# The hand-over from attention to the experts, written out in one order

## The chip, the cores and the metric

The kernel runs on one core of a Trainium2 chip. TensorE (PE) multiplies matrices into PSUM, VectorE (DVE), ScalarE (ACT) and GpSimd (POOL) do the rest, and SyncE (SP) issues most transfers; POOL issues the indirect ones. Each engine works through its own instructions in program order. The metric is the device time of one execution in microseconds (us), lower is better.

## The reference: windowed attention, then a mixture of experts

```python
scores = scale * np.matmul(q, k.transpose(0, 1, 3, 2))     # q, k, v: 8 x 8 heads x 576 x 64
mask = (rel >= 0) & (rel < 64)                             # each row sees itself and 63 before it
attn = softmax(np.where(mask, scores, -1e9));  x = attn @ v  # -> x: 4608 tokens x 512
logits = (x / |x|) @ (emb / |emb|).T / tau                 # 8 experts
expert_idx = np.argmax(logits, axis=1);  gate_w = softmax(logits)[expert_idx]
for e in range(8):                                         # w1[e]: 512 x 1024, w2[e]: 1024 x 512
    h = np.maximum(x[mask] @ w1[e], 0.0)
    out[mask] = gate_w[mask, None] * (h @ w2[e])
```

All is in 32-bit floats.

## The kernel before

Attention runs over 36 tiles of 128 tokens (`T` = 0 to 35). A tile passes through a row of links, and `stages(s)` writes one link of each of several tiles: `scores(s)`, then `own_scores` (ACT), `all_scores` and `maxima` (DVE), `less_max` (POOL), `exponentials` (ACT) of tile s; `attn_transposes` (PE), `attn_own` and `attn_prev` (DVE) of tile s-1; `values` (PE) and `x_out` (DVE) of tile s-2; `x_transposes` (PE), `xT_evac` and `squares` (ACT) of tile s-3; `logits` (PE) of tile s-4. Per group of two or four tiles there follow `logits_out` and `choose` (DVE), the running count of tokens per expert (POOL), `ranks` (PE) and `ranks_out` (DVE). `place(T)` (POOL) then scatters the tile's 128 rows of x into a table in DRAM, sorted by expert. It reads the row buffer `xbuf[T % 8]`, so the next tile that uses this buffer may write to it only when that scatter has landed; the first such write is `tokens(T)` (POOL) or `x_out(T)`.

The experts work on slots of 128 rows, in 21 fixed steps `g` of two slots each (`F`) or one (`H`). Slots 0 and 1 (step 0) and 2 and 3 (step 1) are known to belong to expert 0 and need only the first 24 and 32 tiles. All later slots depend on the counts of all 36 tiles: `cnt = counts(...)`, then some fifty small DVE operations, `slot_rows`, which give `meta` (the expert of a step) and `where` (the rows of a slot). Only then can SP issue `load1(2)`, the 2 MB of `w1` for step 2, and after it the rows of slots 4 and 5 (`load_x`).

A slot's x is loaded (`xb`), turned by DVE (`xt`, `STREAM_TRANSPOSE` x4), rounded by ACT (`xh`), and POOL takes the rest (`xl = xt - xh`). A weight is split in the same way: ACT makes `w1h` from `w1raw`, and DVE `w1l`. `layer1(g, f)` is a piece of 12 matmuls, 128 x 128 by 128 x 256, for f = 0 to 7; two pieces fill a PSUM bank `ph`, from which ACT makes `hh` and DVE `hl`. `layer2(g)` is 48 matmuls with 512 columns.

In what follows the end of attention is the stretch from the last full stage to the first piece of step 2. Before, stage 35 is the last call of `stages`; then `x_parts(0)` and `x_parts(1)`, the links that were left, pieces of step 0 between some of them, the rest of step 0, all of step 1's first layer, `layer2(0)`, and then `step(1)`, whose first work on PE is `layer1` of step 2.

Of the kernel before, what the change touches and what calls it, by code (L numbers as in the profile page):

```python
# [9 lines left out]
F32 = mybir.dt.float32  # L10
# [11 lines left out]
P = 128  # L22
# [63 lines left out]
def attention_moe(ctx, tc, q, k, v, emb, tau, w1, w2, kc, kt, out):  # L86
# [5 lines left out]
    stage_a, stage_p, stage_q = ExitStack(), ExitStack(), ExitStack()  # L92
    ap = stage_a.enter_context(tc.tile_pool(name="ap", bufs=2, side="right"))
    aq = stage_q.enter_context(tc.tile_pool(name="aq", bufs=2))
    psq = stage_q.enter_context(tc.tile_pool(name="psq", bufs=1, space=PSUM))
    psa = stage_p.enter_context(tc.tile_pool(name="psa", bufs=1, space=PSUM, side="right"))

# [17 lines left out]
    turned, score = (psq.tile([P, 2, 512], F32, name=nm) for nm in ("turned", "score"))  # L115
# [101 lines left out]
    vb = [ap.tile([P, 4, NB, D + 1], F32, name=f"v{i}", bufs=1) for i in range(2)]  # L217
# [147 lines left out]
    def choose(G):  # L365
# [13 lines left out]
        for i in range(n):  # L379
            T = a + i  # L380
            nc.gpsimd.tensor_tensor(out=acc[:, T + 1], in0=acc[:, T], in1=oh[:, i], op=ALU.add)
# [11 lines left out]
    def counts(T, name):  # L393

        pn = cnv
        nc.tensor.matmul(pn, lhsT=ones, rhs=acc[:, T], start=True, stop=True)
        o = const.tile([P, E], F32, name=name)
        nc.vector.tensor_copy(o, pn)
        return o
# [83 lines left out]
    def stages(s):  # L483
# [60 lines left out]
        for G in ending(3):  # L544
            choose(G)
        for n, i in todo[1:]:
            keep_chunk(n, i)
# [151 lines left out]
    def shared_rows():  # L699

        ovv = misc[:, 136:136 + SLOTS]
# [25 lines left out]
    def x_parts(a):  # L727

        b, t = xb.pop(a), take("xt")
        o = t.rearrange("p (c t i) -> p t c i", c=4, i=32)  # L730
        bv = b.rearrange("p (t c j) -> p t c j", t=4, j=32)
        for k in range(4):
            nc.vector.transpose(o[:, k], bv[:, k])  # L733
        g, j = POS[a]
        if j == 0:
            xp[g] = take("xh"), take("xl")
        xh, xl = (x[:, :, j * P:(j + 1) * P] for x in xp[g])
        t = t.rearrange("p (c n) -> p c n", c=4)
        nc.scalar.copy(xh, t)  # L739
        nc.gpsimd.tensor_tensor(out=xl, in0=t, in1=xh.bitcast(F32), op=ALU.subtract)  # L740

# [93 lines left out]

    def hidden(g, part):

        if part == 0:
            hp[g] = take("hh"), take("hl")
        hh, hl = (x[:, part * 512:(part + 1) * 512] for x in hp[g])  # L840
        p = ph.pop((g, part))
        nc.scalar.activation(hh, p, AF.Relu)  # L842
# [293 lines left out]
```

## Time and profile before

| what | us |
|---|---|
| median of 3 runs | 677.48 (676.59 to 681.18) |
| the profiled execution | 673.52 |
| its span, first to last instruction | 671.7 |
| PE busy in the span | 638.5 (95%) |
| DVE busy | 463.2 (69%) |
| ACT busy | 392.1 (58%) |
| POOL busy | 204.1 (30%) |

The page divides the span into slices and engines; the trace behind it lists each instruction with its start and length. A matmul's length is modelled and overlaps the next, so what a row of matmuls costs is read from start to start. The share "PEclk" is the TensorE clock that was granted: 1.00 is 2.4 GHz and 0.50 is 1.2 GHz. Idle time is put down to the instruction that ended it.

### The profile page before, as it was taken

The numbers are of one execution on the slowest core, as the hardware profiler recorded it, in microseconds if no ns is written. First come the engines' busy times: TensorE is split into PE (matmuls) and PEld (weight loads), VectorE is DVE, ScalarE is ACT, GpSimd is POOL, SyncE is SP. The second block draws the span as 40 slices with busy tenths as digits, with TensorE's granted clock in tenths as the row PEclk, the third lists the DMA queues.
The fourth block names the chain that finished last, engine by engine and source line by source line (L and its number), as shares of the span: only waits on it lengthen the run. The fifth ranks groups of instructions, "written<-read, shape, count | busy, mean of one in ns | idle before, by whom it ended". The sixth has DMA issues, their size and how long they took to land.

```text
span 671.7 us, 19526 instructions
## 1 busy us (share of the span) xinstructions
PE 638.5 (95%) x7564; PEld 570.9 (85%) x7564; DVE 463.2 (69%) x978; ACT 392.1 (58%) x591; POOL 204.1 (30%) x243
## 2 busy tenths in 40 slices
PE   8899999999978999999999999999999999999991
PEld 7788888887867979988998899998989998999881
DVE  2688898889887885667656877567665776647630
ACT  4587787777653444465546765546565466546640
POOL 0223555544463422222221332222122322231111
PEclk9999999999988999999999999999999999999996
DMA  8999988988372358884688689784797967767221
GB/s 232 228 249 271 257 236 218 229 230 198 103 239 76 129 138 309 280 274 157 228 267 273 220 262 298 218 292 161 250 309 225 291 235 233 238 220 268 101 71 35
DMA packets 122021, 146.86 MB, mean 219 GB/s; under 512 B 52406, under 2 KB 85046, under 8 KB 121921
## 3 DMA queue, kind: packets, MB, share of 16 engines
q1 hardware_dynamic: 115024, 125.19, 63.2%
q0 software_dynamic: 6000, 19.18, 7.5%
q8 instruction: 61, 1.00, 0.7%
q10 hardware_dynamic: 896, 1.18, 0.6%
q14 instruction: 40, 0.32, 0.1%
HBM read 123.09 MB, written 23.20 MB: 218 GB/s over the span
## 4 chain that ended last, share of the span: by engine, by line
PE 71%; DVE 13%; DMA 6%; issue 4%; SPq 2%; ACT 1%; POOL 0%; ACTq 0%; POOLq 0%; DVEq 0%
PE ph L833 28%; PE po L882 28%; PE pair L297 2%; PE turned L183 2%; PE ph L860 2%; PE back L334 2%; PE score L245 2%; DMA raw<-in_q 2%; DVE xr L317 2%; PE pair L302 2%; DVE aP L286 2%; DVE aO L282 1%; PE misc L351 1%; DMA raw<-in_k 1%; SPq L159 1%
## 5 line engine op out<-in xcount | busy, mean ns | idle before, releaser
L833 PE MATMUL ph<-xh,w1l 128*128 128x256 f32 x576 | 164.2, 285 | 1.7 <-DVE w1l L145 1.5
L833 PE MATMUL ph<-xh,w1h 128*128 128x256 f32 x576 | 164.2, 285 | 0.0
L833 PE MATMUL ph<-xl,w1h 128*128 128x256 f32 x576 | 163.7, 284 | 0.0
L882 PE MATMUL po<-w2h,hl 128*128 128x512 f32 x312 | 121.9, 391 | 0.0
L882 PE MATMUL po<-w2h,hh 128*128 128x512 f32 x312 | 121.9, 391 | 0.0
L882 PE MATMUL po<-w2l,hh 128*128 128x512 f32 x312 | 121.8, 390 | 0.0
L843 DVE SCALAR_TENSOR_TENSOR hl<-ph,hh 128x512 fp32r<-128x512 f32 x78 | 53.5, 689 | 98.8 <-ACT hh L842 98.8
L892 POOL DMA_INDIRECT out<-o,rest x39 | 49.8, 1277 | 218.7 <-ACT o L891 205.4
L833 PEld LDWEIGHTS ph<-xh,w1l 128*128 128x128 f32 x576 | 111.3, 193 | 2.5 <-DVE w1l L145 2.5
L145 DVE TENSOR_TENSOR w2l<-w2raw,w2h 128x1024 fp32r<-128x1024 f32 x80 | 94.7, 1220 | 26.7 <-ACT w2h L142 25.1
L833 PEld LDWEIGHTS ph<-xh,w1h 128*128 128x128 f32 x576 | 111.1, 193 | 1.0 <-issue 0.2
L833 PEld LDWEIGHTS ph<-xl,w1h 128*128 128x128 f32 x576 | 111.2, 193 | 0.6
L142 ACT CAST w2h<-w2raw 128x1024 fp32r<-128x1024 f32 x80 | 81.6, 1049 | 47.6 <-PE po L882 35.1
L145 DVE TENSOR_TENSOR w1l<-w1raw,w1h 128x1024 fp32r<-128x1024 f32 x80 | 94.1, 1234 | 10.9 <-ACT w1h L142 10.6
L740 POOL TENSOR_TENSOR xl<-xt,xh 128x512 fp32r<-128x512 f32 x39 | 50.3, 1294 | 111.6 <-ACT xh L739 111.6
L842 ACT ACTIVATE hh<-ph 128x512 fp32r<-128x512 f32 x78 | 45.8, 594 | 58.5 <-PE ph L833 51.0
L142 ACT CAST w1h<-w1raw 128x1024 fp32r<-128x1024 f32 x80 | 78.0, 1048 | 0.0
L882 PEld LDWEIGHTS po<-w2h,hl 128*128 128x128 f32 x312 | 58.6, 188 | 12.3
L882 PEld LDWEIGHTS po<-w2l,hh 128*128 128x128 f32 x312 | 58.6, 188 | 11.8
L882 PEld LDWEIGHTS po<-w2h,hh 128*128 128x128 f32 x312 | 58.7, 188 | 11.7
L265 POOL TENSOR_TENSOR sm<-sm,st 128x512 f32<-128x512 f32 x36 | 37.4, 1040 | 68.4 <-DVE sums L314 22.9
L739 ACT CAST xh<-xt 128x512 fp32r<-128x512 f32 x39 | 24.2, 620 | 56.7 <-DVE xt L733 55.8
(175 smaller groups left out, 1007.8 us busy)
## 6 DMA issues: line engine op xcount, KB each, us to landing
w1raw<-in_moe_w SPq DMA_DIRECT2D x80, 512.0 KB
w2raw<-in_moe_w SPq DMA_DIRECT2D x80, 512.0 KB
xb<-xs SPq DMA_DIRECT2D x156, 64.0 KB
raw<-in_q SPq DMA_DIRECT2D x64, 144.0 KB
v<-in_v SPq DMA_DIRECT2D x64, 144.0 KB
raw<-in_k SPq DMA_DIRECT2D x56, 144.0 KB
xs<-xr SPq DMA_DIRECT2D x12, 264.0 KB
rest<-xs SPq DMA_DIRECT2D x39, 8.0 KB
```

The lines of the kernel that those rows point to most:

```text
L142: nc.scalar.copy(hi[c], raw[c])
L145: eng.tensor_tensor(out=lo[c], in0=raw[c], in1=hi[c].bitcast(F32), op=ALU.subtract)
L183: nc.tensor.transpose(to[:, j // 3, j % 3 * I:(j % 3 + 1) * I], rl[n][:, j, 2 * i:2 * i + 2].rearrange("p h d -> p (h d)"), ident[:I, :I])
L245: nc.tensor.matmul(score[64 * z:64 * z + 64, hp, (u + 1) * P - w:(u + 1) * P], lhsT=qT[b % 2][pr, u, at:at + WIN], rhs=kT[b % 2][pr, u, at ...
L265: nc.gpsimd.tensor_tensor(out=t, in0=t, in1=st.pop(T).unsqueeze(2).to_broadcast([P, 8, WIN]), op=ALU.subtract)
L739: nc.scalar.copy(xh, t)
L740: nc.gpsimd.tensor_tensor(out=xl, in0=t, in1=xh.bitcast(F32), op=ALU.subtract)
L833: nc.tensor.matmul(o, lhsT=ww[c][:, f * P:(f + 1) * P], rhs=xx[:, c, :n], start=(c == 0 and i == 0), stop=(c == 3 and i == 2))
L842: nc.scalar.activation(hh, p, AF.Relu)
L843: nc.vector.scalar_tensor_tensor(out=hl, in0=p, scalar=0.0, in1=hh.bitcast(F32), op0=ALU.max, op1=ALU.subtract)
L882: nc.tensor.matmul(po[a], lhsT=xx[:, f, at], rhs=ww[f // 2][:, f % 2], start=(f == 0 and i == 0), stop=(f == 7 and i == 2))
L892: d = nc.gpsimd.indirect_dma_start(out=out, out_offset=bass.IndirectOffsetOnAxis(ap=tok, axis=0), in_=o, in_offset=None, bounds_check=N - ...
```

## The change

Stage 35 is no longer written by `stages`; the loop ends at stage 34, and all that follows up to `layer2(0)` stands in one order written by hand, in which pieces of `layer1(0)` lie between the links of tiles 33 to 35. Helpers are split so that their parts can be placed alone: `x_parts` into `x_turned`, `x_hi` and `x_lo`, `hidden` into `hidden_hi` and `hidden_lo`, `choose` into `choose` and `count`, `counts` into `sum_counts` and `counts`. The first `xh`, `xl` and the two `xt` have memory from the start, `load_x(0)` and `load_x(1)` are issued one stage earlier, the PSUM banks of `turned` are given up first and those of `score` next, and the memory of V goes to `w2l`. The tile of the shared-rows sum moves to a `ph` bank inside `layer2(0)`.

```diff
-    stage_a, stage_p, stage_q = ExitStack(), ExitStack(), ExitStack()
+    stage_a, stage_v, stage_p, stage_q, stage_s, stage_t = (ExitStack() for _ in range(6))
...
-    for t in range(NT):
+    for name, shape, dtype in (("xh", [P, 4, 2 * P], F32R), ("xl", [P, 4, 2 * P], F32R)):
+        buffers(name, 1, shape, dtype, const)
+    buffers("xt", 2, [P, 512], F32, const)
+    for t in range(NT - 1):
...
-        if t == CUTS[0] + 8:
+        if t == CUTS[0] + 7:
             load_x(0)
             load_x(1)
+    stage_t.close()
...
+    logits(31)
+    squares(32)
+    x_turned(0)
+    place(27)
+    values(33)
+    x_turned(1)
+    x_hi(0)
+    tokens(35)
+    tokens(34)
+    tokens(33)
+    x_transposes(32)
+    logits_out(8)
+    x_lo(0)
+    x_hi(1)
+    choose(8)
+    scores(35)
...
+    x_lo(1)
+    attn_transposes(34)
+    own_scores(35)
+    logits(32)
+    attn_own(34)
+    squares(33)
+    count(8)
+    layer1(0, 0)
+    attn_prev(34)
+    all_scores(35)
...
+    logits(35)
+    x_lo(3)
+    layer1(0, 7)
+    logits_out(10)
+    choose(10)
+    layer1(1, 0)
+    split_lo(2, w2raw, w2h, w2l, nc.vector)
+    count(10)
+    hidden_hi(0, 3)
+    hidden_lo(0, 3)
+    sum_counts(NT)
+    ranks(10)
+    layer1(1, 1)
+    cnt = counts("cnt")
+    ranks_out(10)
+    weave(slot_rows(cnt))
+    load1(2)
...
+    layer2(0, shared_rows)
+    hidden_lo(1, 2)
+    hidden_hi(1, 3)
+    hidden_lo(1, 3)
+    x_turned(5)
+    x_turned(4)
+    weave(gate_logits(0))
+    x_hi(5)
+    x_lo(5)
+    x_hi(4)
+    gate_exp(0)
+    split_hi(0, w1raw, w1h)
+    x_lo(4)
+    split_hi(1, w1raw, w1h)
+    split_lo(0, w1raw, w1h, w1l, nc.vector)
...
+    split_lo(3, w1raw, w1h, w1l, nc.vector)
+    load1(3)
```

The order of POOL at the start of this stretch, before: `L425` is a `place`, `L323` a `tokens`, `L265` a `less_max`, `L381` the running count, `L740` an `x_lo`. The three scatters are those of tiles 26, 28 and 29, the one behind is that of tile 27.

```order
L425 DMA xs<-xr,pi 36992x528 x3
L323 COPY xr<-ct 128x1
L265 TENSOR_TENSOR sm<-sm,st 128x512
L425 DMA xs<-xr,pi 36992x528
L381 TENSOR_TENSOR acc<-acc,oh 128x8 x2
L740 TENSOR_TENSOR xl_4222<-xt_4224,xh_4220 128x4x128
L740 TENSOR_TENSOR xl_4222<-xt_4225,xh_4220 128x4x128
```

And in the changed kernel, where the lines are `L431`, `L326`, `L268`, `L386` and `L756`:

```order
L431 DMA xs<-xr,pi 36992x528 x4
L326 COPY xr<-ct 128x1 x3
L756 TENSOR_TENSOR xl_352<-xt_353,xh_351 128x4x128
L756 TENSOR_TENSOR xl_352<-xt_354,xh_351 128x4x128
L386 TENSOR_TENSOR acc<-acc,oh 128x8 x2
L268 TENSOR_TENSOR sm<-sm,st 128x512
```

The scatter of tile 27 now stands ahead of three `tokens`, of which the first, that of tile 35, writes the same row buffer (27 and 35 leave 3 when divided by 8); both `x_lo` stand behind them, and the count of group 8 and the `less_max` of tile 35 behind those.

The order of PE from the same place, before (`L351` logits, `L334` x_transposes, `L277` attn_transposes, `L245` scores, `L833` a piece's matmul, `L297` and `L302` values):

```order
L245 MATMUL score<-kT_115,qT_113 64x128 x16
L351 MATMUL misc<-embT,xT 64x8 x8
L334 MATMUL back<-cs,xr 128x128 x4
L297 MATMUL pair<-v_117,aO 64x65 x4
...
L277 MATMUL back<-cs,sm 128x128 x4
...
L351 MATMUL misc<-embT,xT 64x8 x8
L833 MATMUL ph_4239<-xh_4220,w1h_99 128x256
L833 MATMUL ph_4239<-xl_4222,w1h_99 128x256
```

And in the changed kernel (`L354`, `L300`, `L305`, `L337`, `L248`, `L280`, `L854`):

```order
L354 MATMUL misc<-embT,xT 64x8 x8
L300 MATMUL pair<-v_123,aO 64x65 x4
L305 MATMUL pair<-v_123,aP 64x65 x4
...
L337 MATMUL back<-cs,xr 128x128 x4
L248 MATMUL score<-kT_121,qT_119 64x128 x16
L280 MATMUL back<-cs,sm 128x128 x4
L354 MATMUL misc<-embT,xT 64x8 x8
L854 MATMUL ph_4130<-xh_351,w1h_105 128x256
L854 MATMUL ph_4130<-xl_352,w1h_105 128x256
```

The scores of tile 35 move behind the values of tile 33, and the first piece of `layer1(0)` stands behind the logits of tile 32, ahead of the values of tile 34 instead of behind them.

The order of DVE at the end of the stretch in the changed kernel, between the turning of slots 5 and 4 and the low halves of step 2's w1 (`L781` to `L797` are `gate_logits`):

```order
L741 STREAM_TRANSPOSE xt_353<-xb_350 128x4x32 x4
L741 STREAM_TRANSPOSE xt_354<-xb_349 128x4x32 x4
L781 TENSOR_REDUCE gsm_4226<-rest 128x4
L783 TENSOR_SCALAR gsm_4227<-gsm_4228 128x4
L785 TENSOR_TENSOR gin_4229<-rest,gsm_4226 128x32
...
L797 TENSOR_TENSOR gin_4229<-gin_4229,gsm_4228 128x32
L148 TENSOR_TENSOR w1l_109<-w1raw_97,w1h_105 128x1024
```

And of ACT there, where `L802` is `gate_exp`:

```order
L752 CAST xh_351<-xt_353 128x4x128
L752 CAST xh_351<-xt_354 128x4x128
L802 ACTIVATE gin_4229<-gin_4229 128x32
L145 CAST w1h_105<-w1raw_97 128x1024
L145 CAST w1h_106<-w1raw_98 128x1024
```

Before, DVE turns the two slots and begins with `w1l` at once, ACT goes from `xh` to `w1h`, and `gate_logits` and `gate_exp` of batch 0 lie among the `hidden` of step 1, ahead of all this.

## Rows read from the trace of the kernel before

**Rows 1.** Busy time by stretch: us busy (instructions) per engine, clock, DMA share, GB/s.
```profile
180.00:220.00 40.00, 33.19 (x732) 28.81 (x725) 31.12 (x104) 16.77 (x35) 21.28 (x38) 0.87 0.46 145
197.70:225.70 28.00, 25.31 (x385) 22.95 (x386) 20.20 (x74) 9.52 (x20) 14.61 (x22) 0.83 0.31 99
260.00:280.00 20.00, 20.00 (x126) 18.09 (x125) 13.30 (x21) 11.77 (x15) 4.86 (x4) 1.00 0.76 244
```

**Rows 2.** Timeline of PE: start, length, what, in brackets idle time before.
```profile
197.79 1.12 PE L334 MATMUL back<-cs,xr 128*128 128x128 f32 x4 [1.17 <-DVE aP L286]
209.04 0.39 PE L833 MATMUL ph<-xh,w1h 128*128 128x256 f32 x1
...
212.02 0.60 PE L334 MATMUL back<-cs,xr 128*128 128x128 f32 x4
...
213.12 0.35 PE L297 MATMUL pair<-v,aO 64*64 64x65 f32 x8
...
214.21 0.39 PE L833 MATMUL ph<-xh,w1h 128*128 128x256 f32 x1
...
237.44 0.39 PE L882 MATMUL po<-w2h,hh 128*128 128x512 f32 x1
...
248.13 0.39 PE L882 MATMUL po<-w2h,hl 128*128 128x512 f32 x1
```

**Rows 3.** Single microseconds in which the granted clock changed, columns as in Rows 1.
```profile
197.00:198.00 1.00, 0.21 (x1) 0.22 (x2) 1.00 (x4) 0.10 (x1) 0.69 (x2) 0.56 0.33 131
207.00:208.00 1.00, 0.51 (x4) 0.25 (x2) 0.93 (x3) 0.15 (x2) 1.00 (x2) 0.82 0.00 0
251.00:252.00 1.00, 0.62 (x3) 0.42 (x3) 1.00 (x2) 0.00 (x0) 1.00 (x1) 0.86 0.36 74
255.00:256.00 1.00, 1.00 (x9) 1.00 (x9) 0.00 (x0) 0.60 (x1) 0.00 (x0) 0.93 0.76 274
```

**Rows 4.** Timeline of POOL.
```profile
198.72 0.98 POOL L425 DMA_INDIRECT xs<-xr,pi  x1 [0.30 <-issue]
199.69 0.20 POOL L323 COPY xr<-ct 128x1 int32<-128x1 int32 x1
...
205.83 2.50 POOL L740 TENSOR_TENSOR xl<-xt,xh 128x512 fp32r<-128x512 f32 x2 [1.00 <-ACT xh L739]
...
222.65 2.56 POOL L740 TENSOR_TENSOR xl<-xt,xh 128x512 fp32r<-128x512 f32 x2 [1.51 <-ACT xh L739]
```

**Rows 5.** The ten scatters from 195 to 230 us, from issue to landing.
```profile
DMA to landing us min/median/max: 2.8/2.8/4.3
```

**Rows 6.** Timeline of DVE, and of ACT for `gate_exp`.
```profile
204.21 1.66 DVE L733 STREAM_TRANSPOSE xt<-xb 128x128 f32<-128x128 f32 x8
...
222.85 1.13 DVE L416 TENSOR_TENSOR rk<-rk,oh 128x16 f32<-128x16 f32 x1
...
224.22 1.01 DVE L420 CAST pi<-pos 128x2 int32<-128x2 f32 x1
...
225.74 0.14 DVE L619 TENSOR_TENSOR cnt<-cnt,shift 128x1 f32<-128x1 f32 x1
...
233.68 4.61 DVE L145 TENSOR_TENSOR w2l<-w2raw,w2h 128x1024 fp32r<-128x1024 f32 x4
...
238.82 0.17 DVE L760 TENSOR_REDUCE gsm<-rest 128x4 f32<-128x32 f32 x1
...
240.37 0.23 ACT L781 ACTIVATE gin<-gin 128x32 f32<-128x32 f32 x1 [5.41 <-DVE gin L776]
```

**Rows 7.** Transfers issued by SP: start, time of the issues, what.
```profile
231.47 2.52 SPq L804 DMA_DIRECT2D w1raw<-in_moe_w  x4
```

**Rows 8.** The chain that ended last, in order of time: start, length, what.
```profile
241.12 1.89 DMA xb<-xs
...
245.89 0.96 ACT w1h L142
246.87 5.36 DVE w1l L145 x4
```

More of the change, by code (lines that the diff above doesn't have):

```diff
@@ L545, in stages @@
             choose(G)
+            count(G)
         for n, i in todo[1:]:
@@ L1013, in attention_moe @@
     ring([io.tile([P, DM], F32, name=f"xb{i}") for i in (2, 3)] + rings["xb"][1], "xb")
-    psm = ctx.enter_context(tc.tile_pool(name="psm", bufs=1, space=PSUM, reuse_waits="tile"))
-    ring([psm.tile([P, 512], F32, name=f"ph{i}") for i in range(4)], "ph")
-    T, G = NT - 1, len(GROUPS) - 1
-    x_transposes(T - 2)
-    values(T - 1)
-    xT_evac(T - 2)
-    x_parts(0)
-    x_parts(1)
-    ranks(G - 2)
-    attn_transposes(T)
-    ranks_out(G - 2)
-    begin_late(1, counts(CUTS[1], "early2"))
@@ L1027, in attention_moe @@
-    place(T - 5)
-    place(T - 4)
-    load_x(2)
+    w2h += [io.tile([P, 2, DM], F32R, name=f"w2h{c}") for c in range(4)]
+    xT_evac(32)
+    x_out(33)
+    x_lo(1)
[8 more added lines that the diff above has]
+    all_scores(35)
+    stage_s.close()
+    psm2 = ctx.enter_context(tc.tile_pool(name="psm2", bufs=1, space=PSUM, reuse_waits="tile"))
+    more = [psm2.tile([P, 512], F32, name=f"ph{i}") for i in (2, 3)]
@@ new lines, in attention_moe @@
+    ranks(8)
+    values(34)
+    maxima(35)
+    ranks_out(8)
+    less_max(35)
+    x_transposes(33)
+    x_out(34)
+    sum_counts(CUTS[1])
+    layer1(0, 1)
+    xT_evac(33)
+    place(30)
+    exponentials(35)
+    begin_late(1, counts("early2"))
+    squares(34)
+    logits(33)
+    place(31)
+    attn_transposes(35)
+    hidden_hi(0, 0)
+    logits_out(9)
+    layer1(0, 2)
+    choose(9)
+    attn_own(35)
+    count(9)
+    layer1(0, 3)
+    attn_prev(35)
+    hidden_lo(0, 0)
+    ranks(9)
@@ L1030, in attention_moe @@
+    values(35)
+    stage_v.close()
+    iob = ctx.enter_context(tc.tile_pool(name="iob", bufs=1, reuse_waits="tile"))
+    w2l += [iob.tile([P, 2, DM], F32R, name=f"w2l{c}") for c in range(4)]
+    load_x(2)
+    hidden_hi(0, 1)
+    ranks_out(9)
+    x_transposes(34)
+    hidden_lo(0, 1)
+    place(32)
+    split_hi(0, w2raw, w2h)
+    ring(more + rings["ph"][1], "ph")
+    layer1(0, 4)
+    x_out(35)
     load_x(3)
     load_rest(*range(EARLY))
-    x_out(T - 1)
-    tokens(T - 1)
-    attn_own(T)
@@ L1080, in attention_moe @@
-    w2l += [io2.tile([P, 2, DM], F32R, name=f"w2l{c}") for c in range(4)]
-    buffers("o", 4, [P, DM], F32, io2)
-    buffers("hr", 2, [P, 512], F32, io2)
-    load1(2)
+    xT_evac(34)
+    place(33)
+    x_turned(2)
+    split_hi(1, w2raw, w2h)
+    layer1(0, 5)
+    split_lo(0, w2raw, w2h, w2l, nc.vector)
+    squares(35)
+    x_transposes(35)
+    x_hi(2)
+    logits(34)
+    x_turned(3)
+    hidden_hi(0, 2)
+    x_lo(2)
+    layer1(0, 6)
+    xT_evac(35)
+    hidden_lo(0, 2)
+    x_hi(3)
```

160 lines of the change are left out of this document (77 added, 83 removed).

## Prediction, before the changed kernel was run

> **What bounds the kernel now.** I read the page's busy shares first, then busy time by stretch, then the timelines of single engines around the one weak stretch, and last the chain of waits. From 260 us on PE is busy all the time at the full clock [rows 1], and the page's slices show the same until the tail: whatever makes step 2 begin earlier or later moves the end of the kernel by as much, and nothing later can give it back. The reader is to see two weak places ahead of that. Between 180 and 220 us PE is busy for 33.19 of 40 us, at a mean clock of 0.87 [rows 1]. It waits for DVE's aP, for 1.17 us before 197.79 alone [rows 2]; the clock falls to 1.2 GHz after such idle time, at about 197.1, and is back at 2.4 GHz at about 207.4 [rows 3]. The second place is the start of step 2. PE issues the last of layer2(0)'s 48 matmuls at 248.13 [rows 2], and the chain goes on with PE only behind the low halves of w1, which end at 252.2 [rows 8]; the clock is low once more from about 251.7 to 255.1 [rows 3].
>
> The chain of waits says what sets this second place: not PE. The counts of all 36 tiles are out and the slot list begins on DVE at 225.74 [rows 6]; w1 of step 2 is issued at 231.47 [rows 7], 5.73 us later; its transfer and behind it the rows of slots 4 and 5 have landed at 241.12 + 1.89 = 243.01; then DVE turns them, ACT rounds them, ACT splits w1 and DVE ends the fourth low half at 246.87 + 5.36 = 252.23 [rows 8]. So two questions decide the time: when does the slot list begin, and what stands between the landing of the rows and the fourth low half?
>
> **The start of the slot list.** PE now has nine pieces of the first layer ahead of the last count instead of fewer, so it is PE's row of work that sets the time, once it can begin. It can begin when POOL has made the xl of both slots. In POOL's order four scatters come first. The third begins at 198.72, one takes 0.98 and 0.30 of issue [rows 4], so the fourth, tile 27's, begins at 200.0. Behind it stands the token copy of tile 35, which writes the buffer that this scatter reads; a scatter takes 2.8 us to land [rows 5], hence 202.8. Three copies at 0.20, overlapped a little, make 0.5, and two xl 2.50 [rows 4]: 205.8. What queues behind that wait on POOL is the count of group 8 and the less_max of tile 35; the first is needed by PE behind piece 0, the second on the way to tile 35's exponentials, and both come out in time for PE's order by these lengths. DVE can turn x from 197.7 on, when aP is out [rows 2], so that is no limit. The earlier x loads pass SP's queue ahead of the last two w2 transfers; those are not used before ACT's first w2h, well behind the pieces, which hides it; if that cover were gone, the price would be one wait of ACT for w2.
>
> From 205.8 on PE has: nine pieces at half of 212.02 - 209.04 = 2.98 each, 13.4; two values at 214.21 - 213.12 = 1.09; three times x_transposes with logits at 213.12 - 212.02 = 1.10; one attn_transposes at half of that; the small rank matmuls 0.1 [rows 2]. That is 13.4 + 2.2 + 3.3 + 0.5 + 0.1 = 19.5, so the last count leaves PE at 225.3. DVE copies it and makes group 10's ranks, five small operations at some 0.17 each (nine of such size take 240.37 - 238.82 = 1.55 [rows 6]): the list begins at 226.2, **0.5 us later** than before. PE has by then done one piece more than before, 1.5 us, but that is not on the path.
>
> The bounds of this term: DVE's own work is the lower one. From 197.7 to 225.7 it is busy 20.20 us [rows 1]. The change adds three w2 low halves at 4.61/4 [rows 6], 3.5 in all, and can take away what two operations beside xl cost too much, 0.96 + 0.84 (below): 21.9, hence 219.6 at the earliest, 6.1 us sooner. Above, I take one more stall of PE of the size of a scatter's landing, 2.8: +3.3. I stay with 0.5, near the middle, since each of its parts has a row.
>
> **From the landed rows to the fourth low half.** The list's shift goes on unchanged through load and landing: same transfers, same order on SP. Before, the rest takes 252.23 - 243.01 = 9.2. Now DVE turns both slots, 1.66; then come the nine gate operations, 1.55, that used to lie far ahead; ACT's exponential, 0.23, stands ahead of w1h in ACT's order; w1h 0.98 from start to start, then four low halves at 4.61 in all [rows 6, 8]: 9.0. To this comes a new neighbour. POOL's two xl run at the same time as the gate operations. Beside two such xl at 222.65 [rows 4], DVE's rank product took 1.13 and the cast behind it 1.01, each ending as an xl ended, where the like take 0.17 [rows 6]: 0.96 + 0.84 = 1.8 us lost. I take those 1.8, as the nearest row: 10.8, **1.6 us later**. The ends are 0 and all of both xl, 2.56: -0.2 to +2.4.
>
> The Trainium skill (SBUF — State Buffer, "Who interferes with whom") has a rule for this: a DVE operation with two inputs in SBUF, and a GpSimd one that reads SBUF, share one port, and the second to issue waits for the whole of the first. By the rule alone the term would be up to 2.56 instead of 1.8, and the whole sum 0.8 us higher; the two slow rows ended where the xl ended, which agrees.
>
> **The rest.** The clock: PE ends layer2(0) at about 225.3 + 7 pieces (10.4) + layer2(0) as before (237.44 to 248.13 and one matmul more [rows 2], 10.9) = 246.6, and then waits some 6 us, longer than before. It will fall to 1.2 GHz there as before and come back after 3.4 us [rows 3]; I take no difference, with bounds of -1.7 (it doesn't fall, half of 3.4) and +1.7 (it stays low for a second such stretch). The moved PSUM banks and memory add no instruction; their waits are for work that ended long before. Later w2 and w1 loads are issued no later than before relative to step 2.
>
> **Sum:** 0.5 + 1.6 + 0 = +2.1. The profiled execution took 673.52, so 675.6; the median of the runs lies 3.96 above it, at 677.48, hence **679.6**. All lower bounds together: -6.1 - 0.2 - 1.7 = -8.0; all upper ones: +3.3 + 2.4 + 1.7 = +7.4.
>
> **Rivals.** *The cover works.* The wait behind the scatter is short, or DVE instead of PE sets the list, which begins at its earliest, 6.1 us sooner, and the gate operations meet no xl (-0.2): 677.48 - 6.3 = **671.2**. For it: DVE is free for 8 of the 28 us behind 197.7 [rows 1], and PE's lost time there is there to be filled. Against it: POOL's order as above, and nine pieces that PE must do before the count.
>
> *The clock stays low under the first pieces.* With tile 35's scores moved back, PE has one link less ahead of the values of tile 33, so more idle time there than before, and it waits again for xl up to 205.8. Before, the clock stayed low for 10.3 us, 197.1 to 207.4 [rows 3]. If it now stays low until 211, the 5.2 us of PE work after 205.8 run at half rate and lose 2.6; if the longer wait at step 2 brings a second low stretch, 1.7 more. 2.1 + 2.6 + 1.7 = 6.4: **683.9**, slower. It decides at 206 us: a clock of 1.00 there excludes it. Against it: PE has values, transposes, scores and logits without a pause from 197.8 on, and in the rows the clock came back in such work.
>
> *The order changes what PE does but not the load.* If w1 and the rows land no sooner or later than before (the list begins at 225.7) and no operation is held, only the place of the gate operations remains, -0.2: **677.3**, no change.
>
> **How the numbers follow.** My forecast has 0.50, the cover 0.20, the low clock 0.15, no effect 0.15. One per cent, 6.8 us, is about what a measurement here can tell from no change, so faster means under 670.7 and slower over 684.3. The cover reaches 671.2 and with a clock that never falls 669.5, so somewhat under half of it counts as faster, and a little for what I don't see: 0.10. Of the low clock somewhat under half lies beyond 684.3, and of the forecast's upper tail a tenth: 0.12. The rest, 0.78, is no change. For 8 in 10 I leave out the far ends of both rivals: 671 to 684.5; the forecast's own range is 676 to 683.
>
> **What would show it.** Right: POOL's token copy ends its wait some 2.8 us after the fourth scatter began; the second matmul of the first piece waits for xl until about 206; PE has no wait over 0.5 us from there to the last count near 225; the slot list begins within 1.5 us of 226; of the nine gate operations two are near 1 us; w1h begins behind the exponential; and PE stands idle for some 6 us ahead of step 2, at a clock that falls. Wrong: a slot list that begins before 223, xl ready before 203, a clock of 0.50 after 207, or a PE that reaches step 2 without waiting for w1l. The whole forecast falls if the rows of slots 4 and 5 don't land about 17 us after the list begins.

## The result: 1.4% slower, where 0.3% was forecast

| | us |
|---|---|
| median before, in the same group of runs | 677.93 (676.59 to 681.18) |
| median of the changed kernel | 687.87 (686.20 to 689.47) |
| ratio | 1.0139, 95% interval 1.0094 to 1.0184 |
| profiled execution of the changed kernel | 688.63, span 686.8 |

That is 9.9 us more (6 to 12 by the interval), against 2.1 forecast. The two profiled executions lie 15.1 us apart, so they overstate it: in the unchanged stages DVE began the last low half of w1 at 195.77 us here and at 192.10 before, 3.7 us that are not of the change (below, a kernel with the old program up to there, but for two loads issued one stage earlier, stood at 198.75). I therefore count each event from that low half, in both.

| stretch | before | after | difference | forecast |
|---|---|---|---|---|
| last low half of attention's w1 to slot list | 33.64 | 39.91 | +6.3 | +0.5 |
| slot list to the end of the fourth low half | 26.5 | 28.8 | +2.3 | +1.6 |
| from there to the last matmul | 405.2 | 408.4 | +3.2 | 0 |

The differences add up to 11.8 us, within what the ratio allows. Counting from the low half doesn't remove all that varies from execution to execution. In the four profiles below with the old order up to the list (before, b_misaligned, b_w1_first, b_x01) the list stands 33.6, 35.5, 36.3 and 38.5 us behind the low half; in the five with the changed order (the changed kernel, after_placed, w1_first, after_aligned, gate_late) 39.9, 39.1, 40.0, 40.1 and 42.8. Between the means lie 4.4 us, so the change makes the list later by more than the forecast's 0.5, but the +6.3 of one pair is not its exact price.

### The stretch ahead of the slot list

Busy time in the weak stretch that the forecast began with, in the changed kernel (columns as in [rows 1]). The kernel's program is 3.7 us later here, so the second line is the stretch that matches the forecast's:

```profile
180.00:220.00 40.00, 33.19 (x718) 28.30 (x717) 29.98 (x97) 16.16 (x35) 20.98 (x38) 0.87 0.39 137
183.67:223.67 40.00, 33.03 (x681) 28.54 (x678) 30.90 (x104) 17.55 (x35) 21.32 (x38) 0.87 0.41 138
```

PE is busy for 33.03 of 40 us there, against 33.19 before, at the same mean clock: what lies between the links now filled none of its idle time. POOL's timeline from the fourth scatter on answers to [rows 4] (start, length, what, in brackets idle time before):

```profile
203.68 0.98 POOL L431 DMA_INDIRECT xs<-xr,pi  x1 [0.30 <-issue]
206.59 0.42 POOL L326 COPY xr<-ct 128x1 int32<-128x1 int32 x3 [1.92 <-DMA xs<-xr,pi]
206.97 2.48 POOL L756 TENSOR_TENSOR xl<-xt,xh 128x512 fp32r<-128x512 f32 x2
...
221.90 0.99 POOL L431 DMA_INDIRECT xs<-xr,pi  x1 [2.17 <-DVE pi L426]
...
230.29 2.10 POOL L756 TENSOR_TENSOR xl<-xt,xh 128x512 fp32r<-128x512 f32 x1 [3.94 <-ACT xh L752]
233.26 1.32 POOL L386 TENSOR_TENSOR acc<-acc,oh 128x8 bf16<-128x8 bf16 x2 [0.87 <-DVE oh L381]
```

The token copies ended their wait 2.91 us behind the start of the fourth scatter, and both xl were ready at 209.45, 13.7 us behind the low half: the forecast's 205.8, counted from 192.10, is 13.7 too. POOL's row was read rightly. But PE wasn't there. Its timeline in values(33) and at the waits further on; in the kernel before PE had no wait of this kind between 212 us and its last count at 221.18:

```profile
201.96 0.44 PE L305 MATMUL pair<-v,aP 64*64 64x65 f32 x8
202.18 0.85 PE L300 MATMUL pair<-v,aO 64*64 64x65 f32 x8
203.28 0.46 PE L305 MATMUL pair<-v,aP 64*64 64x65 f32 x2 [0.26 <-issue]
204.02 0.52 PE L305 MATMUL pair<-v,aP 64*64 64x65 f32 x4 [0.28 <-issue]
205.45 0.26 PE L305 MATMUL pair<-v,aP 64*64 64x65 f32 x1 [0.92 <-issue]
...
211.00 0.38 PE L854 MATMUL ph<-xh,w1h 128*128 128x256 f32 x1
...
230.27 0.38 PE L854 MATMUL ph<-xh,w1h 128*128 128x256 f32 x1 [0.60 <-ACT xh L752]
232.44 0.38 PE L854 MATMUL ph<-xl,w1h 128*128 128x256 f32 x1 [1.79 <-POOL xl L756]
234.64 0.17 PE L400 MATMUL misc<-acc,ones 128*128 128x8 bf16 x1 [0.63 <-POOL acc L386]
```

First, matmuls of values(33) come in small numbers with pauses put down to "issue": PE waited for nothing that the profile shows. From its first matmul (200.87) to the next operation (206.19) it took 5.3 us; a kernel without the pauses took 2.3 at the same 1.2 GHz (below). So the first piece began at 211.00, 1.5 us behind the xl. Second, from the piece's second matmul at 211.22 to the last count at 234.64 lie 23.4 us instead of the forecast's 19.5. The waits at 230.27, 232.44 and 234.64 take 3.6 of that, from start to start; without them PE's work was 19.8 us, nearly as forecast. The chain of waits says what the first two hang on:

```profile
221.90 3.22 DMA xs<-xr,pi
225.14 0.31 SPq L726
...
226.44 2.05 DMA xb<-xs
...
228.67 0.89 DVE xt L741 x4
```

The rows of slot 3 were issued only when the scatter of tile 32 had landed. They need the first 32 tiles and not this one; but `load_x(3)` now stands behind `place(32)` in the written order, and its read of the table was held until this scatter's landing (221.90 + 3.22 = 225.12; SP's row begins at 225.14). Before, both loads stood ahead of that scatter. The third wait is for POOL's running count, which begins only when DVE's oh is out (POOL's last line above). Behind these waits the clock fell to 1.2 GHz once more, from about 234.5 to 238.0 (columns as in [rows 1]; the third last is the clock):

```profile
235.00:236.00 1.00, 1.00 (x6) 1.00 (x6) 0.86 (x7) 0.00 (x0) 0.00 (x0) 0.50 0.00 0
```

### From the slot list to step 2, and behind it

DVE's timeline there, against [rows 6] (gate operations) and [rows 8]:

```profile
253.60 1.65 DVE L741 STREAM_TRANSPOSE xt<-xb 128x128 f32<-128x128 f32 x8
255.17 0.14 DVE L781 TENSOR_REDUCE gsm<-rest 128x4 f32<-128x32 f32 x1
255.24 1.30 DVE L783 TENSOR_SCALAR gsm<-gsm 128x4 f32<-128x4 f32 x1
...
256.78 1.02 DVE L789 TENSOR_TENSOR gsm<-rest,gsm 128x4 f32<-128x4 f32 x1
```

From turning the rows to the end of the fourth low half it took 264.51 - 253.60 = 10.9 us, before 252.23 - 243.58 = 8.65 [rows 8]. Two gate operations took 1.30 and 1.02 beside the two xl, where the kernel with these operations moved needs 0.15 and 0.16 (gate_late, below): 2.0 us lost, 1.8 forecast. The forecast had 10.8 for these 10.9; the 0.7 by which the step came out larger is that its sum began at the landing, here at 252.94, while DVE, still at hl, begins to turn 0.66 us later, as it did before (0.57). The clock fell as forecast too, and stayed low until 268.6, longer than in [rows 3]:

```profile
262.00:263.00 1.00, 0.71 (x3) 0.71 (x3) 1.00 (x2) 0.68 (x1) 0.00 (x0) 0.50 1.06 361
268.00:269.00 1.00, 1.00 (x7) 1.00 (x7) 0.57 (x1) 0.40 (x1) 0.98 (x2) 0.62 1.04 389
```

4.0 us of step 2 ran at 1.2 GHz instead of 2.8, which costs 0.6 (half of the 1.2 us more). Last, something that no step named: layer2's matmuls are longer. The page's groups (count, busy us, mean ns), before and then after:

```profile
L882 PE MATMUL po<-w2l,hh 128*128 128x512 f32 x312 | 121.8, 390 | 0.0
```

```profile
L913 PE MATMUL po<-w2l,hh 128*128 128x512 f32 x312 | 122.9, 394 | 0.0
```

From the first matmul of layer2(1) to the start of the last matmul of all, with PE never idle, that makes 393.63 us before (263.82 to 657.45) and 396.30 after (276.61 to 672.91): **+2.7 us**. For the share of the placement in it see below.

### The profile page after: what moved, and what is told of

Read it like the earlier page. It is cut to its first block, busy times and chain, and to the rows that moved or that the text cites. A ratio compares the mean times of both kernels' runs of the same rounds, so it can differ in the third digit from the quotient of the medians.

```text
span 686.8 us, 19515 instructions
## 1 busy us (share of the span) xinstructions
PE 646.5 (94%) x7564; PEld 573.1 (83%) x7564; DVE 463.8 (68%) x978; ACT 393.4 (57%) x591; POOL 205.4 (30%) x243
## 4 chain that ended last, share of the span: by engine, by line
PE 72%; DVE 13%; issue 5%; DMA 5%; ACT 2%; POOL 1%; SPq 1%; DVEq 0%; POOLq 0%; ACTq 0%
PE po L913 28%; PE ph L854 27%; PE turned L186 3%; PE score L248 3%; PE pair L300 2%; PE ph L891 2%; PE back L337 2%; PE misc L354 2%; PE pair L305 2%; DVE xr L320 1%; DVE st L264 1%; DVE sm L260 1%; PE back L280 1%; DVE aP L289 1%; DMA raw<-in_k 1%
## 5 line engine op out<-in xcount | busy, mean ns | idle before, releaser
L854 PE MATMUL ph<-xh,w1h 128*128 128x256 f32 x576 | 164.9, 286 | 2.6 <-ACT w1h L145 2.0
L854 PE MATMUL ph<-xh,w1l 128*128 128x256 f32 x576 | 164.6, 286 | 1.5 <-DVE w1l L148 1.3
L854 PE MATMUL ph<-xl,w1h 128*128 128x256 f32 x576 | 164.1, 285 | 1.8 <-POOL xl L756 1.8
L913 PE MATMUL po<-w2h,hh 128*128 128x512 f32 x312 | 123.4, 395 | 0.0
L854 PEld LDWEIGHTS ph<-xh,w1h 128*128 128x128 f32 x576 | 111.4, 193 | 3.9 <-ACT w1h L145 2.4
L854 PEld LDWEIGHTS ph<-xl,w1h 128*128 128x128 f32 x576 | 111.3, 193 | 2.7 <-POOL xl L756 2.0
L854 PEld LDWEIGHTS ph<-xh,w1l 128*128 128x128 f32 x576 | 111.3, 193 | 2.5 <-DVE w1l L148 2.5
L756 POOL TENSOR_TENSOR xl<-xt,xh 128x512 fp32r<-128x512 f32 x39 | 51.4, 1319 | 110.9 <-ACT xh L752 110.9
L913 PEld LDWEIGHTS po<-w2h,hl 128*128 128x128 f32 x312 | 58.5, 188 | 13.9
L268 POOL TENSOR_TENSOR sm<-sm,st 128x512 f32<-128x512 f32 x36 | 37.4, 1040 | 74.4 <-DVE sums L317 24.4
```

The source lines that it names most:

```text
L268: nc.gpsimd.tensor_tensor(out=t, in0=t, in1=st.pop(T).unsqueeze(2).to_broadcast([P, 8, WIN]), op=ALU.subtract)
L854: nc.tensor.matmul(o, lhsT=ww[c][:, f * P:(f + 1) * P], rhs=xx[:, c, :n], start=(c == 0 and i == 0), stop=(c == 3 and i == 2))
L913: nc.tensor.matmul(po[a], lhsT=xx[:, f, at], rhs=ww[f // 2][:, f % 2], start=(f == 0 and i == 0), stop=(f == 7 and i == 2))
```

## The experiments

They ran in five groups; each group was on one chip, beside runs of the kernel before. All ratios are to that kernel, with the 95% interval; a difference of two ratios is one between groups, unless both kernels stood in one. Diffs are to the changed kernel unless said otherwise.

### Was it the scatter of tile 32?

**x3_early**

```diff
     load_x(2)
+    load_x(3)
+    load_rest(*range(EARLY))
...
     x_out(35)
-    load_x(3)
-    load_rest(*range(EARLY))
```

> load_x(3) and load_rest moved from behind place(32) to right behind load_x(2). Theory (the read of slot 3 waits for the scatter of tile 32, which it does not need): the last four x transfers land some 3 us after the first four, xl of slot 3 is ready by about 227 instead of 232.4, PE's waits of 0.60, 1.79 and 0.63 us between 229.7 and 234.6 go, the slot list begins 2.5 to 3.0 us earlier relative to the first piece of step 0, and the time falls by as much: 685. Rival (the list is late because of what lies ahead of the first piece, and something else fills the 3 us): list and time stay within 0.7 us of the changed kernel's.

1.0055 (1.0027 to 1.0083), so 0.84% or 5.7 us less than the changed kernel, whose runs stood in another group; 2.5 to 3.0 were expected. SP issued all eight x transfers in 5.02 us (8.03 in the changed kernel), and of PE's three waits only the one for the count stayed (first SP's timeline, then PE's waits between 218 and 240 us: in all, times, longest):

```profile
217.33 5.02 SPq L726 DMA_DIRECT2D xb<-xs  x8
```

```profile
PE misc L400 <- POOL acc L386: 0.6, 1, 0.6
```

Counted from the low half, the last count came 2.4 us earlier and the last matmul 3.5. The theory holds for the first two waits; the third, for the count, has another cause. **x3_placed** repeats it in another group, with the memory as before (after_placed, below).

> The changed kernel with load_x(3) and load_rest ahead of place(32), and w2h and w2l placed as in the kernel before. Theory (two separate losses): 3 to 5 us less than with the placement alone (1.008), a ratio of 1.001 to 1.004, layer2 at 390 ns. Rival: 1.006 or more. Scatters as in the changed kernel: pauses in values(33), if this call has them.

1.0018 (0.9994 to 1.0042) against after_placed's 1.0080 (1.0053 to 1.0106): 0.6%, 4.2 us, and the intervals don't overlap.

### Was it the order at the end?

**gate_late**

```diff
     x_turned(4)
-    weave(gate_logits(0))
     x_hi(5)
     x_lo(5)
     x_hi(4)
-    gate_exp(0)
...
     split_lo(3, w1raw, w1h, w1l, nc.vector)
+    weave(gate_logits(0))
+    gate_exp(0)
     load1(3)
```

> The nine gate operations and the exponential of step 0 moved from ahead of the split of w1 to behind it, nothing else. Theory (they lie on the path between the landed rows and the fourth low half, held by the two xl): the first w1h begins at the end of xh instead of 2.8 us later, and the time falls by 2.8 to 3.5 us, to about 684.5. Rival (the two xl hold w1's first low half instead, since it too has two inputs in SBUF): the first low half takes 2 us or more and the gain is under 2 us.

1.0094 (1.0059 to 1.0130). That is 0.45% under the changed kernel's 1.0139, but in another group and with intervals that overlap, and its last matmul lies no nearer to the low half (477.6 us, changed kernel 477.1), since its list began later, 42.8 us behind it. So the time shows no gain, and the theory rests on the stretch alone. DVE, from the turning to the two gate operations that were held:

```profile
255.38 1.66 DVE L741 STREAM_TRANSPOSE xt<-xb 128x128 f32<-128x128 f32 x8 [0.83 <-DMA xb<-xs]
258.67 5.35 DVE L148 TENSOR_TENSOR w1l<-w1raw,w1h 128x1024 fp32r<-128x1024 f32 x4 [1.64 <-ACT w1h L145]
264.04 0.15 DVE L783 TENSOR_SCALAR gsm<-gsm 128x4 f32<-128x4 f32 x1
264.47 0.16 DVE L789 TENSOR_TENSOR gsm<-rest,gsm 128x4 f32<-128x4 f32 x1
```

264.02 - 255.38 = 8.64 us, what the kernel before needed: the whole of the 2.3 was the gate operations. Now the four low halves take 5.35, as they did before [rows 8] (5.36), where they took 4.64 in the changed kernel. The Trainium skill (SBUF — State Buffer, "Who interferes with whom") says that who issues first, not the kind of operation, decides who is held. This agrees with it as far as one profile goes: with the gate operations away, the operations that are longer are those that now run beside the xl.

**w1_first** (`sum_shared` is the matmul of `shared_rows` alone, which now makes only the comparison)

```diff
-    layer2(0, shared_rows)
+    layer2(0, sum_shared)
     hidden_lo(1, 2)
     hidden_hi(1, 3)
     hidden_lo(1, 3)
+    for c in range(4):
+        split_hi(c, w1raw, w1h)
+        split_lo(c, w1raw, w1h, w1l, nc.vector)
+    load1(3)
     x_turned(5)
     x_turned(4)
...
+    shared_rows()
+    weave(gate_logits(0))
+    gate_exp(0)
```

> The last part of the changed kernel rearranged: w1 of step 2 is split as its quarters land, ahead of turning the rows of slots 4 and 5; DVE's comparison for shared rows and the gate operations come behind. Theory (the chain from the landing of w1 at 250.6 to step 2 at 264.6 is DVE's and ACT's order, not the transfers): the fourth low half ends within 2.5 us of w1's landing, x parts are ready some 4 us after the rows land, PE goes from layer2(0) into step 2 with less than 1 us of idle and at the full clock: 7 us from the idle time and 2 us from the clock, 679. Rival (the transfers set it: the rows land late and the whole of the turning and rounding still stands behind them): a gain under 4 us, with PE idle for over 3 us.

1.0018 (0.9984 to 1.0052): 1.2%, 8 us less, and in its profile the last matmul lies 469.8 us behind the low half instead of 477.1. Its chain from the last count on is PE alone:

```profile
235.85 11.65 PE ph L858 x84
247.50 5.55 PE po L917 x24
253.06 0.13 PE ph L710
253.19 5.75 PE po L917 x24
258.94 3.08 PE ph L858 x26
```

So the 6.6 us from the end of layer2(0) to the fourth low half (257.92 to 264.51), of which PE is idle for 3.4, hung on the order of DVE and ACT and not on the transfers; the forecast took them over from the kernel before as given. **both** joins x3_early's and w1_first's diffs, and **b_w1_first** makes the same move in the kernel before:

```diff
-    x_parts(4)
-    x_parts(5)
     renew(w1raw, w1h, w1l)
     load1(3)
+    x_parts(4)
+    x_parts(5)
```

> The two orders that helped, together: load_x(3) and load_rest ahead of place(32), and w1 of step 2 split ahead of the rows of slots 4 and 5. Theory (two separate losses: PE's three waits ahead of the last count, and the end of the chain to step 2): PE goes from the last count to the end without idle, and 3.0 us (the waits) to 5.7 us (what the first order gained by itself) come on top of the gain of the second: a ratio of 0.993 to 0.997 to the kernel before. Rival (both shorten the same idle time ahead of step 2): no gain over the second order alone, 1.000 to 1.003.

> The kernel before with one edit: w1 of step 2 is split (and load1(3) issued) ahead of turning the rows of slots 4 and 5, instead of behind. Theory (there too DVE's and ACT's order holds step 2, since w1 lands 1.9 us ahead of the rows and each quarter of it earlier): PE's idle time of some 4 us ahead of step 2 and the low clock behind it shrink, 3.5 to 5 us faster, a ratio of 0.993 to 0.995. Rival (DVE has three w2 halves, the gate operations and four hl in that stretch, and the split can't begin before the last piece of step 1 has read w1): under 2 us, 0.997 or more.

both: 0.9989 (0.9965 to 1.0012), no slower than before, but short of the 0.993 to 0.997 that was expected. Against w1_first, in another group, it is 0.3% less, inside the intervals, so the times don't show that the two gains add. The profiles agree with it: the last matmul lies 465.8 us behind the low half, 11.3 us less than in the changed kernel, where x3_early has 3.5 and w1_first 7.3. b_w1_first: 1.0014 (0.9979 to 1.0050), nothing gained, the rival. There DVE had w2 halves, hl and gate operations until 246.5 us; w1 was split behind them, the rows turned behind that, and step 2 waited for xl:

```profile
249.92 1.22 DVE w1l L145
251.14 0.81 DVE xt L733 x4
...
253.90 1.27 POOL xl L740
```

This suggests that the order pays only because the change does three of the four w2 halves ahead of the slot list, which would be one thing that it gains; no run takes these halves alone back.

### What holds the first piece?

**both_scores** and **both_place27**, each to "both":

```diff
+    scores(35)
     logits(31)
...
     choose(8)
-    scores(35)
```

```diff
-    place(27)
     values(33)
...
-    tokens(35)
-    tokens(34)
-    tokens(33)
...
     x_lo(1)
+    place(27)
+    tokens(33)
+    tokens(34)
...
     less_max(35)
+    tokens(35)
```

> The kernel with both orders, and scores(35) moved from behind choose(8) to ahead of logits(31), where PE waits 2 us for DVE's ranks. Theory (the time ahead of the first piece is PE's: idle, then at 1.2 GHz): the scores run in that wait, the clock is back at 2.4 GHz earlier, the first piece of step 0 begins 2 to 4 us earlier after the last low half of w1 than with both orders alone, and the time falls by as much. Rival (POOL's row with the token copies and xl holds the first piece at that same point): the first piece waits for xl, less than 1 us gained.

> The kernel with both orders, and place(27) with the three token copies moved on POOL from ahead of xl of slots 0 and 1 to behind it (the copy of tile 35 behind less_max(35)). Theory A (PE's matmuls of values(33) come in fours 0.7 us apart because its instructions arrive late behind the scatters): with three scatters instead of four in flight these pauses end about 1.3 us earlier, and the first piece begins 1.3 us earlier. Theory B (the pauses have a length of their own): they last 2.5 us as before, xl is ready 3 us earlier and nothing waits for it: less than 0.5 us gained. The prediction's step (POOL's wait for the scatter of tile 27 holds the first piece) would give 3 us.

0.9986 (0.9951 to 1.0022) and 0.9988 (0.9959 to 1.0016): neither gained. In this group no profile had pauses in values(33), so theories A and B of the second weren't tested. With the scatter of tile 27 moved, the piece's second matmul came 1.9 us earlier in the profile (12.3 us behind the low half, in both 14.2) and the list 1.2 earlier, but the time stayed; the prediction's step would have given 3 us. With "both", PE now did wait for xl, 2.08 us at the piece's second matmul. With the scores moved it was there earlier and waited longer:

```profile
203.54 0.58 PE L858 MATMUL ph<-xh,w1h 128*128 128x256 f32 x1
208.83 0.58 PE L858 MATMUL ph<-xl,w1h 128*128 128x256 f32 x1 [4.71 <-POOL xl L760]
```

This is the forecast's own step, POOL's wait for the scatter (3.95 us in this kernel), once PE is in time. The changed order itself shows it in after_placed (below), whose profile has no pauses:

```profile
205.70 0.38 PE L854 MATMUL ph<-xl,w1h 128*128 128x256 f32 x1 [1.62 <-POOL xl L756]
```

That is 13.9 us behind the low half, as forecast and 1.5 earlier than in the changed kernel, and yet the list came only 0.8 earlier (39.1): the waits behind it were there, and PE fell to 1.2 GHz again under the first pieces (0.50 from 207 to 209 us). So in that profile the list was late without any pauses. **all** makes all four moves.

> Both orders, the scores of tile 35 ahead of logits(31), and place(27) with the token copies behind the two xl. Theory (with both orders PE sets all from the first piece on; that piece waited for xl where only the scores were moved, and for PE's own work where only the scatter was): each alone gained nothing since the other held it, together the first piece begins 1.5 to 4 us earlier than with both orders alone, ratio 0.993 to 0.997. Rival (xl is held by ACT and DVE, or PE by xT of tile 32): less than 1 us earlier.

0.9965 (0.9935 to 0.9996), in the range expected. The first piece came less early than expected: its second matmul 13.5 us behind the low half, in both 14.2, and the list, at 37.7, no earlier than there (36.2). Its group had the pauses again.

### Where do layer2's matmuls lose?

By the addresses in the built programs, w2h and w2l of the kernel before start 32 bytes ahead of a multiple of 4,096, in the changed kernel 128 and 800 behind one. **b_misaligned** (to the kernel before) puts both at 128 behind; **after_aligned** puts w2h alone where it was relative to such a multiple; **all_aligned** does that to "all"; **after_placed** and **all_placed** put both back so.

```diff
+    io2.tile([P, 40], F32, name="space0")
     w2h += [io2.tile([P, 2, DM], F32R, name=f"w2h{c}") for c in range(4)]
     w2l += [io2.tile([P, 2, DM], F32R, name=f"w2l{c}") for c in range(4)]
+    io2.tile([P, 984], F32, name="space")
```

```diff
     rest = io.tile([P, SLOTS, ROW - DM], F32, name="rest")
+    io.tile([P, 16], F32, name="space")
+    w2h += [io.tile([P, 2, DM], F32R, name=f"w2h{c}") for c in range(4)]
...
+    iob.tile([P, 800], F32, name="space2")
     w2l += [iob.tile([P, 2, DM], F32R, name=f"w2l{c}") for c in range(4)]
```

The first is b_misaligned, whose two spaces make 4,096 bytes, so that what is allocated behind w2 keeps its place relative to such a multiple; of the second, the two kernels with w2h alone have no space2.

> The kernel before with one edit: w2h and w2l lie 3,936 bytes lower, so 128 bytes behind a multiple of 4,096, as w2h does in the changed kernel; nothing else in its order. Theory (where w2h and w2l lie sets the matmul): 394 ns instead of 390 in layer2, 2 to 4 us slower. Rival: 390 ns as before, no change.

> The changed kernel with one edit: w2h stands 4,256 bytes lower in memory, 32 bytes ahead of a multiple of 4,096 as in the kernel before, instead of 128 behind one; w2l stays nearly where the change put it. Theory (layer2's matmuls take 394 ns instead of 390, and 231 instead of 227 ns from start to start, in every profile of the changed kernel, because of where w2h and w2l lie): the matmuls that read w2h fall back to 390 ns and those of w2l stay at 394, and from step 2 to the end some 1.6 of the 2.4 us that were lost come back. Rival (it is hh and hl, or traffic): all three forms stay at 394 ns. The time alone can't tell this. It also shows once more how long values(33) takes: 4.8 us with pauses, or 2.2 us without, as in the runs with both orders.

> As the one before, with w2h where the kernel before had it relative to 4,096. Theory: a further 1.6 us faster, the same times as in its neighbour up to step 2. Rival: no difference.

> The changed kernel with w2h and w2l both 32 bytes ahead of a multiple of 4,096, as in the kernel before; nothing else. Theory (the place of both sets layer2's matmuls): 390 ns and 227 ns from start to start in all three forms, and some 3 us less from step 2 to the end than the changed kernel, a ratio of 1.007 to 1.011. Rival (hh and hl, which the change also moved, or the traffic beside it): 394 ns or more, a ratio of 1.011 to 1.014.

> The kernel with all four moves, and w2h and w2l both placed as in the kernel before. Theory: 390 ns, and 3 us less than the four moves alone, a ratio of 0.991 to 0.994. Rival: no difference, 0.996 to 0.998.

The pages' groups of b_misaligned, after_aligned and after_placed:

```profile
L882 PE MATMUL po<-w2l,hh 128*128 128x512 f32 x312 | 123.7, 396 | 0.0
```

```profile
L913 PE MATMUL po<-w2h,hh 128*128 128x512 f32 x312 | 124.2, 398 | 0.0
L913 PE MATMUL po<-w2l,hh 128*128 128x512 f32 x312 | 123.2, 395 | 0.0
L913 PE MATMUL po<-w2h,hl 128*128 128x512 f32 x312 | 122.5, 392 | 0.0
```

```profile
L913 PE MATMUL po<-w2l,hh 128*128 128x512 f32 x312 | 121.6, 390 | 0.0
```

| | layer2(1) to the last matmul, us | ratio |
|---|---|---|
| before | 393.63 | 1 |
| b_misaligned | 399.40 | 1.0075 (1.0046 to 1.0104) |
| changed kernel | 396.30 | 1.0139 (1.0094 to 1.0184) |
| after_aligned | 396.76 | 1.0115 (1.0057 to 1.0172) |
| after_placed | 391.53 | 1.0080 (1.0053 to 1.0106) |
| all | 396.31 | 0.9965 (0.9935 to 0.9996) |
| all_aligned | 396.56 | 0.9982 (0.9949 to 1.0015) |
| all_placed | 391.54 | **0.9896 (0.9871 to 0.9920)** |

No order differs within these comparisons, so the place of w2h and w2l in memory alone moves this stretch by 5.8 us in the kernel before, which became 0.75% slower. In the changed kernel it is worth 4.8 us (396.30 - 391.53) and not the 2.7 seen above: with both tiles back the stretch is 2.1 us shorter than before, because layer1's matmuls come about 118.5 ns apart there and 119.9 before. Why they do is not shown. That moving w2h alone would mend its two forms was wrong (398 and 392 ns); with both tiles moved back all three forms were at 390. Which property of the addresses counts is open. The times of the changed kernel and after_placed are of different groups and overlap a little; within one group all_scat and all_scat_placed (below) differ by 0.6% without overlap. all_placed is the version that beats both kernels, by 1.0% and, between groups, 2.4%.

### What are the pauses in values(33)?

**all_scat** and **all_scat_placed** (to "all" and "all_placed") and **after_scat** (to the changed kernel) take the scatters out of that stretch:

```diff
-                if s == (T + 8 if b - a == 4 else b + 4):
+                if s == (T + 8 if b - a == 4 else b + 4) and T not in (26, 28, 29):
...
     x_lo(1)
+    place(26)
+    place(27)
+    tokens(33)
...
     count(8)
+    place(28)
...
     less_max(35)
+    place(29)
+    tokens(34)
+    tokens(35)
```

> The kernel with all four moves, and the scatters of tiles 26, 28 and 29 moved on POOL from ahead of the xl of slots 0 and 1 to behind them, so that none is in flight while PE does values(33). Theory A (the pauses of 0.7 us in values(33) come from the scatters): no pauses there, values(33) takes 1.1 to 2.2 us instead of 3.5 to 4.8, and with xl made 3 us earlier the first piece begins 2 to 4 us earlier. Theory B (these matmuls or their place in the program cause them): pauses as before, 1.5 to 2.5 us in sum. In the run on which no kernel had pauses none would show here either, and then only the earlier xl remains.

> The two together: the moved scatters and the placed w2h and w2l. Theory: the gains add, 2 to 5 us less than with all four moves, a ratio of 0.989 to 0.993. Rival (one or both give nothing): 0.996 or more.

> The changed kernel with the scatters of tiles 26, 27, 28 and 29 and the token copies behind the two xl; nothing else. Theory A (scatters cause the pauses): no pauses in values(33) even if its neighbour has them; the first piece begins 2.4 us earlier then. Theory B (the matmuls or their place in the program): pauses as in its neighbour. If neither has them, the xl are 3 us earlier and the first piece begins when PE has done its links: 0 to 2 us.

all_scat: 0.9958 (0.9927 to 0.9989); all_scat_placed: 0.9897 (0.9872 to 0.9922), the same as all_placed in that group, so moving these scatters gained nothing. No profile of their group had pauses, with scatters or without, so they decide nothing on A and B. after_scat's group does. Its neighbour x3_placed, with the scatters, has pauses in values(33):

```profile
203.03 0.36 PE L300 MATMUL pair<-v,aO 64*64 64x65 f32 x1 [0.36 <-issue]
...
203.78 0.46 PE L305 MATMUL pair<-v,aP 64*64 64x65 f32 x3 [0.26 <-issue]
205.21 0.37 PE L305 MATMUL pair<-v,aP 64*64 64x65 f32 x2 [0.96 <-issue]
```

after_scat has none there; one stands in values(34), behind the scatters that now begin at 210.51 and 211.81:

```profile
207.04 0.46 PE L305 MATMUL pair<-v,aP 64*64 64x65 f32 x8
...
215.30 0.37 PE L305 MATMUL pair<-v,aP 64*64 64x65 f32 x5 [0.44 <-issue]
```

This agrees with theory A, but it is one pair of profiles, and scatters are not enough: in two of the five groups no profile had pauses in values(33), in the three others every descendant of the changed kernel with these scatters in their place did. Nor are the pauses the change's alone. b_x01 (below), with the order of before, has them too:

```profile
206.37 0.38 PE L302 MATMUL pair<-v,aP 64*64 64x65 f32 x2 [0.26 <-issue]
207.10 0.39 PE L302 MATMUL pair<-v,aP 64*64 64x65 f32 x3 [0.36 <-issue]
```

What passes between the scatters and PE is not shown. That PE's instructions come late, as theory A of both_place27 has it, is one rival that no run tests by itself. In after_scat the piece's second matmul came 11.2 us behind the low half, 4.3 earlier than in the changed kernel where 2.4 was expected, and the list 38.0, 1.9 earlier. Its time, 1.0107 (1.0075 to 1.0140), can't be told from the changed kernel's.

### Were the earlier loads to blame?

**b_x01** (to the kernel before):

```diff
-        if t == CUTS[0] + 8:
+        if t == CUTS[0] + 7:
             load_x(0)
```

> The kernel before with one part of the change alone: the rows of slots 0 and 1 are loaded one stage earlier. Theory: these loads were never waited for, so the time is that of before within 0.7 us, and stage by stage the first 190 us look as in the changed kernel's other runs. Rival (two transfers issued ahead of the scatters and of the last w2 transfers delay those): 1 to 4 us slower. If the profile of this kernel is some 3 to 4 us late by stage 34 without the rest of the change, as the changed kernel's is, then that part of the difference between the two profiles is from execution to execution.

0.9991 (0.9963 to 1.0020): no cost. Its profile stood at 198.75 us at the low half, later than any other, with the program of before otherwise, and its list came 38.5 us behind it, with a clock of 1.2 GHz for some 17 us there instead of 10: both vary from execution to execution.

## Why the prediction was wrong, step by step

- **The start of the slot list, +0.5: the step that failed**, by 5.8 us in this pair of profiles (by 3.9 between the means of all). POOL's row (xl 13.7 us behind the low half) and PE's work (19.8 us against 19.5) were right. That "it is PE's row of work that sets the time, once it can begin", with no wait over 0.5 us, was not: the text looked at the moved scatter of tile 27 and what waits behind it, but not at that of tile 32, whose `load_x(3)` stands a few lines below it in the kernel. PE waited for the rows of slot 3 instead, and once more for the count: three waits, 3.6 us in the profile. x3_early took away the first two, and with them 2.4 us off the list and 3.5 off the last matmul.
- Another 1.8 us there, from the xl to the piece's second matmul, came from PE itself: the pauses, 3.0 us, which lay partly beside POOL's wait. The text said against the rival of the low clock that PE has work "without a pause from 197.8 on", and no row of before showed such a pause; b_x01 shows that they are not peculiar to the change. What causes them stays open.
- **The rival of the low clock** lies nearest to the result with its 683.9, but by another way: in this profile the clock was low under values(33) and back some 15 us behind the low half in both kernels. It fell once more behind the waits for slot 3, from 234.5 to 238.0, which is past the last count. In after_placed, where PE did wait for xl, its mechanism occurred in part: about 3 us at 1.2 GHz under the first pieces, and so some 1.5 us lost.
- **Landed rows to the fourth low half, +1.6:** right in mechanism, 2.3 in size, inside the upper bound of 2.4. The two operations lost 2.0, against 1.8 by the row. By the rule of the Trainium skill (SBUF — State Buffer, "Who interferes with whom") they would have lost up to 2.56, which is further off; that the step as a whole would then come to 2.4, nearer to the measured 2.3, is luck, since the 0.7 above the forecast comes from the wait between landing and turning, which its sum left out (0.66 here, 0.57 before). One of the two held operations, the TENSOR_SCALAR of 1.30, has a single input in SBUF, so the rule as the forecast gave it, for two inputs, doesn't cover what this trace shows.
- **Clock, 0:** +0.6, within its bounds.
- **"The moved PSUM banks and memory add no instruction":** true, and yet 2.7 us, since the same matmuls ran slower. This term was missing.
- **The idle time ahead of step 2** was forecast at some 6 us, though the forecast's own terms make 252.2 + 2.1 - 246.6 = 7.7. The stretch was 6.6, with PE idle for 3.4 of it, but it was taken as fixed; w1_first shows that 7 to 8 us could be had there.

Of the other signs of being right, the second matmul did not wait for xl and the list did not begin within 1.5 us of 226; of those of being wrong, a clock of 0.50 after 207 came. The rest came as written: rows of slots 4 and 5 landed 17.3 us behind the start of the list, and w1h began (258.81) behind the exponential (258.68).

## What to carry to other kernels

When an order is written by hand, list for every load that is moved, or that something is moved past, each store to the same memory that now stands ahead of it: a dependence that the data don't need is as real as one that they do. When buffers move, compare the mean time of unchanged instructions in a stretch without idle time first, ahead of any chain: a shift of a per cent there is worth as much as a wait. And two profiled executions may differ by more than the change; count from the last event that both share, and look at several profiles even then.

## What was not expected of the hardware

The same 128 x 128 by 128 x 512 matmuls ran at a mean of 390 to 398 ns by the place of w2h and w2l in memory, the same within 0.02 us over 393.63 us in three profiles of the old placement. In profiles of some groups, small matmuls paused for 0.3 to 0.9 us each while scatters of POOL were in flight, with nothing to wait for that the profile shows; kernels with the order of before had them too, in one profile of four.
